# A streaming decode kernel: six transfers joined to their neighbours

## The chip, the cores and the metric

One core of one Trainium2 chip runs the whole program; the other cores are not used. The metric is the device time of one execution in microseconds (us). Everything is float32. The core's engines are TensorE (PE in the profile, PEld for its weight loads), VectorE (DVE), ScalarE (ACT), GpSimd (POOL) and SyncE (SP); SP's queue issues all large transfers from HBM to the on-chip buffer.

## The reference

Four sequences, one new token each, width 640. Two attention layers and two MLPs alternate, and both attention layers use the same weights and caches, as both MLPs do:

```
x = x + A(layernorm(x))      # layer one
x = x + B(layernorm(x))
x = x + A(layernorm(x))      # layer two, same W_q, K, V, W_o
x = x + B(layernorm(x))

A(x):  q = x @ wq                       # 640 -> 32 heads of 128
       k, v = the last 1024 cached positions of each head
       p = softmax(q k^T / sqrt(128));  o = p v
       return o @ wo                    # 4096 -> 640
B(x):  return (relu(x @ W_gate) * (x @ W_up)) @ W_down   # 640 -> 1728 -> 640
```

Keys and values differ for each of the four sequences, so each element of the caches is used once in a layer. A layer's caches and weights don't fit on the chip together, so nearly all of them are read from HBM twice.

## The kernel before

**One buffer, one stream.** `store` is one tile of 128 partitions by 50624 columns. The inputs lie in HBM as three matrices of 128 rows: `heads` (what 27 heads need, 255744 columns: W_q, K, V and W_o in the order of use), `kept` (the same for the other five heads, 47360 columns) and `mlp` (25920 columns). A load copies a stretch of columns of one of them to a place in `store`; one column is 512 bytes. The heads are worked off in nine groups (`HEADS`: six of four, two of three, one of two). The last two groups, K0 and K1 (heads 27 to 29, and 30 and 31), are the five kept heads: they are done last in layer one, stay in `store` while the MLP's weights pass through what is free, and are done first in layer two, where they are not read again.

**The plan.** `plan` is a list of loads written out by `put` and `stretch` when the program is made: matrix, columns from and to, place. It holds, in this order: the common heads of layer one; with them, at column 3200 of `store`, the 3200 columns of W_q of the kept heads (`put(0, "kept", KEPT * D, ...)`, line 164), then the last three loads of common heads (line 165); the kept heads; the MLP of layer one, in a ring of small places (`gu` twice, `gu_end`, `wd`, lines 170 to 178); the first loads of layer two, into places that the kept heads leave (lines 182 to 189); the common heads of layer two (lines 191 to 203); its MLP in eight loads (`cuts`, line 204). No load is wider than `MOST`, 16320 columns.

**What sets the order.** All loads are issued by SP in the order of the plan. `load()` issues the next one at the point in the program at which `done` has marked its whole place as free; on the chip SP then waits until PE has truly read what lay there. Eight semaphores are used in turn for these loads, so that a load also waits for the landing of the one eight before it. PE goes through its matrix products in program order, each reading a stretch of `store` once that stretch's load has landed: a load is one unit, and none of it counts as there before the last byte is.

**An attention layer** (`attention`) interleaves groups: totals and transposed probabilities of group g, the query of the group after next (`query`), scores of the next group (`scores`), the output projection of the group before (`project`), values of g (`values`). All matrix products go through `product`, line 252: `m` is a query, `ps` scores, `po` values, `y` the residual stream, `pp` the MLP's gate and up columns. An MLP (`forward`) computes the hidden columns in four tiles, `gate(3)`, `gate(0)`, `gate(1)`, `gate(2)` (1920, 5120, 5120 and 5120 columns of the matrix), with the activation `gated` between them, then `down(3)`, `down(0)`, `down(1)`, `down(2)`.

Of the kernel before, what the change touches and what calls it, by code (L numbers as in the profile page):

```python
# [13 lines left out]
B, D, H, DH, W, F = 4, 640, 32, 128, 1024, 1728  # L14
# [17 lines left out]
KEPT = len(HEADS[K0]) + len(HEADS[K1])  # L32
# [19 lines left out]
GU0, GU = KC * 3 * P, KC * 4 * 256  # L52
WD0 = GU0 + 3 * GU
TAIL, WD1, WD = WD0 + D, WD0 + D + 2 * QUARTER, 4 * D
MLP = WD1 + 3 * WD
# [6 lines left out]
STORE = 50624  # L62
FRONT = KEPT * 2 * (D + KV)


AHEAD = KEPT * D, KEPT * D + 768
BACK = FRONT - 2 * KV - 1728, FRONT - 2 * KV
AWAY = BACK[0] - 1280, BACK[0]
HOME = 12864
FIRST, MOST = 32640, 16320  # L70
# [7 lines left out]
def fewest(lo, end, n):  # L78

    if n == 1:  # L80
        return (0, [end]) if end - lo <= MOST else (n + len(CUTS), [])
    most = min(lo + MOST, end)
    ends = [(most, most not in CUTS)] + [(x, False) for x in CUTS if most - 512 < x < most]
    return min((fewest(hi, end, n - 1)[0] + cut, [hi, *fewest(hi, end, n - 1)[1]]) for hi, cut in ends)


def spread(parts):


    at, places, cuts = 0, {}, [0]  # L90
    for what, i in parts:
        places[what, i] = at
        size = size_of(what, i)
        step = {"q": size // KC, "k": 512, "v": 512, "o": D}[what]
        cuts += range(at + step, at + size + 1, step)
        at += size
    return places, at, cuts


ROWS = {row: spread(parts) for row, parts in PARTS.items()}  # L100

CUTS = frozenset(ROWS["heads"][2])
fewest = cache(fewest)
WHERE = {part: (row, at) for row, (places, _, _) in ROWS.items() for part, at in places.items()}

# [2 lines left out]
def decode_kernel(ctx: ExitStack, tc: tile.TileContext, x, source, sel, out):  # L108
    nc = tc.nc
# [10 lines left out]
    store = big.tile([P, STORE], F32, name="store")  # L120
# [9 lines left out]
    def put(layer, row, to, *cuts):  # L130

        for lo, hi in zip(cuts, cuts[1:]):
            assert 0 < hi - lo <= MOST and to % 64 == lo % 64 == hi % 64 == 0 and to + hi - lo <= STORE, (row, lo, hi, to)
            plan.append((layer, row, lo, hi, to))
            to += hi - lo
        return to

    def stretch(layer, lo, end, to):

        for hi in fewest(lo, end, -(-(end - lo) // MOST))[1]:  # L140
            if to + hi - lo > LAP:
                to = 0
            to = put(layer, "heads", to, lo, hi)
            lo = hi
        return to
# [4 lines left out]
    def near(c, row="heads"):  # L150

        return max(x for x in ROWS[row][2] if x <= c)

    heads_end = ROWS["heads"][1]
# [3 lines left out]

    q_end = 2 * KEPT * D
    turn = min(c for c in ROWS["heads"][2] if c >= heads_end - (STORE - q_end))  # L160
    mid = [near(turn + (heads_end - turn) * i // 3) for i in (1, 2)]
    to = stretch(0, HELD, turn, FIRST)
    assert to <= KEPT * D or to > 2 * MOST, to
    put(0, "kept", KEPT * D, KEPT * D, q_end)
    put(0, "heads", q_end, turn, *mid, heads_end)
    put(0, "kept", k0, k0, k1, v0, v0 + 6656, v1, v1 + KV, v1 + 7168, FRONT)
    put(0, "kept", 0, 0, len(HEADS[K0]) * D, KEPT * D)


    f, z, a, q, k = FRONT, STORE - D, AHEAD[0], AWAY[0], BACK[0]  # L170
    assert STORE - FRONT == 2 * 1280 + 64 + D
    gu = [(z, D), (f, 1280), (f + 1280, 1344), (a, 768), (k, 960), (k + 960, 768), (q, 1280)]
    gu_end = [(f, 1280), (f + 1280, 1280), (f + 2560, D)]
    wd = [(a, D), (k, 960), (k + 960, D), (q, 1280), *gu_end, (a, D), (k, D), (k + D, D)]
    lo = 0
    for to, n in gu + gu + gu_end + wd:
        put(0, "mlp", to, lo, lo + n)
        lo += n
    assert lo == MLP
# [2 lines left out]
    lo = HELD  # L182
# [1 line left out]
        put(1, "heads", to, lo, lo + n)  # L184
        lo += n
    to = AHEAD[1]
    for n in 1152, 1280, 1024, 2048, 3392:
        to = put(1, "heads", to, lo, lo + n)
        lo += n
    assert to == HOME  # L190
    to = HOME + BACK[1] - BACK[0]
    for n in 4096, 6144, 9728:
        hi = near(lo + n)
        to = put(1, "heads", to, lo, hi)
        lo = hi
    hi = near(lo + 4608)
    to = put(1, "heads", to, lo, hi)
    lo, hi = hi, near(hi + STORE - to)
    put(1, "heads", to, lo, hi)
    last = near(heads_end - 25216)  # L200
    to = stretch(1, hi, last, 0)
    for lo, hi in (last, near(last + 12800)), (near(last + 12800), heads_end):
        to = put(1, "heads", to if to + hi - lo <= STORE else 0, lo, hi)
    cuts = [0, 7040, 12160, GU0 + 3 * GU, WD1 + WD, MLP - 4 * D, MLP - 2 * D, MLP - D, MLP]
    for lo, hi in zip(cuts, cuts[1:]):
        to = put(1, "mlp", to if to + hi - lo <= STORE else 0, lo, hi)

# [2 lines left out]
    live = [False] * STORE  # L210
    held = {}

    def load():

        if not held:
            nc.sync.dma_start(out=first_q, in_=source["heads"][:, :HELD])
        while plan and not any(live[plan[-1][4]:plan[-1][4] + plan[-1][3] - plan[-1][2]]):
            layer, row, lo, hi, to = plan.pop()
            live[to:to + hi - lo] = [True] * (hi - lo)
            held.setdefault((layer, row), []).append((lo, hi - lo, to))  # L220
            nc.sync.dma_start(out=store[:, to:to + hi - lo], in_=source[row][:, lo:hi])

    def free(a, b):
        live[a:b] = [False] * (b - a)
        load()
# [29 lines left out]
    def done(layer, row, lo, n):  # L255

        if row == "kept" and layer == 0:
            return
        if row == "kept":
            for p in range(lo, lo + n):  # L260
                if BACK[0] <= p < BACK[1]:
                    live[HOME + p - BACK[0]] = False
                elif not (AHEAD[0] <= p < AHEAD[1] or HOME <= p < HOME + BACK[1] - BACK[0]):
                    live[p] = False
        else:
            for first, m, p in held[key(layer, row)]:
                a, b = max(lo, first) - first, min(lo + n, first + m) - first
                if a < b:
                    live[p + a:p + b] = [False] * (b - a)
        load()  # L270
# [8 lines left out]

    probs = work.tile([P, W], F32, name="probs")  # L280
    load()
    gates = work.tile([P, 512], F32, name="gates")
    sel_sb = const.tile([P, P + 32], F32, name="sel_sb")
# [390 lines left out]
```

## Time and profile before

| | |
|---|---|
| median of 3 runs | 732.04 us (731.85 to 732.34) |
| span of the profiled execution, first to last instruction | 729.8 us |
| what lies around the span, by the median | 2.2 us |
| PE busy | 437.2 us (60%) |
| DVE busy, ACT busy | 76.7 us (11%), 54.2 us (7%) |
| transfers of SP's queue | 310.56 MB |
| mean rate over the span | 426 GB/s |
| mean granted TensorE clock | 0.822 |

The profiled execution gives a span; its own time is taken as the span and the 2.2 us around it, which is the median. The spread of the three runs is 0.5 us, 0.07%.

In rows of the timeline the columns are start, duration, engine, source line, operation, output and inputs, partitions and elements, count; in brackets the engine's idle time before the row and what ended it. In a row on a transfer the last number is the time from its issue to its landing. Four bytes times 128 partitions make 512 bytes a column, so 640 columns are 320 KB.

### The profile page before, as it was taken

The page shows a single profiled execution, that of the slowest core. Times are in us where ns is not written, and L with a number is a line of the kernel's source. Part 1 is how long each engine was busy: PE and PEld are TensorE (multiplying, and loading weights), DVE is VectorE, ACT ScalarE, POOL GpSimd, SP SyncE. Part 2 cuts the span into 40 slices and gives each one's busy share as a digit, 9 for nine tenths or more (in the row PEclk, how much of TensorE's full clock was granted, in tenths as well). Part 3 has the DMA queues.
Part 4 walks back from the last instruction along what each step waited for, and adds up shares of the span by engine and source line. Part 5 has one row for each costly group of instructions (what it writes and reads, how often), then busy time and mean ns, then how long its engine had stood idle before and what let it go on. Part 6 is the DMA issues. An engine that isn't in the chain of part 4 may idle for free.

```text
span 729.8 us, 8270 instructions
## 1 busy us (share of the span) xinstructions
PE 437.2 (60%) x3764; PEld 143.9 (20%) x3764; DVE 76.7 (11%) x277; ACT 54.2 (7%) x101; POOL 0.3 (0%) x5
## 2 busy tenths in 40 slices
PE   0745565555646664619868896365656556555575
PEld 0211111111111111103333241021111112111132
DVE  1111001010010101001111211001010010101011
ACT  0200000000000000000412210000000000000100
POOL 0000000000000000000000000000000000000000
PEclk9888888876777777759999999677777777878899
DMA  9999999999999999999999999999999999999996
GB/s 409 442 398 443 442 443 416 438 440 439 418 439 432 411 460 421 447 416 426 419 407 401 434 429 449 445 425 435 425 435 443 429 434 427 441 433 430 421 425 289
DMA packets 13290, 311.17 MB, mean 426 GB/s; under 512 B 1476, under 2 KB 1732, under 8 KB 6984
## 3 DMA queue, kind: packets, MB, share of 16 engines
q1 hardware_dynamic: 13104, 310.56, 99.0%
q8 instruction: 29, 0.48, 0.2%
q10 hardware_dynamic: 152, 0.09, 0.1%
q14 instruction: 5, 0.04, 0.0%
HBM read 310.57 MB, written 0.08 MB: 426 GB/s over the span
## 4 chain that ended last, share of the span: by engine, by line
DMA 76%; PE 21%; another core or an unknown queue 1%; DVE 1%; issue 1%; SPq 0%; ACT 0%; DVEq 0%; ACTq 0%
DMA store<-in_heads 60%; PE ps L252 9%; DMA store<-in_kept 8%; DMA store<-in_mlp 7%; PE po L252 5%; PE m L252 2%; PE y L252 1%; PE pp L252 1%; PE pp L432 1%; PE m L403 1%; PE m L472 0%; PE m L463 0%; PE m L345 0%; PE y L375 0%
## 5 line engine op out<-in xcount | busy, mean ns | idle before, releaser
L252 PE MATMUL po<-store,pT 128*16 128x512 f32 (+1 forms) x1026 | 155.3, 709 | 123.6 <-DMA store<-in_heads 118.2
L252 PE MATMUL ps<-store,qT 128*4 128x512 f32 (+4 forms) x996 | 150.4, 684 | 109.8 <-DMA store<-in_heads 89.2
L252 PEld LDWEIGHTS po<-store,pT 128*16 128x16 f32 x1026 | 34.2, 109 | 230.3 <-issue 109.2
L252 PEld LDWEIGHTS ps<-store,qT 128*4 128x4 f32 x996 | 29.9, 93 | 213.4 <-DMA store<-in_heads 100.3
L424 DVE TENSOR_REDUCE nm<-ps 128x1 f32<-128x1024 f32 x17 | 20.8, 1225 | 240.7 <-PE ps L252 240.7
L428 ACT ACTIVATE probs<-ps,nm 128x1024 f32<-128x1024 f32 x17 | 18.9, 1114 | 327.0 <-DVE nm L424 327.0
L252 PE MATMUL m<-store,xT 128*32 128x512 f32 (+4 forms) x150 | 28.4, 570 | 11.0 <-DMA store<-in_heads 11.0
L442 DVE COPY pT<-pp 128x16 f32<-128x16 f32 x128 | 17.1, 169 | 137.8 <-PE po L252 137.8
L252 PE MATMUL y<-store,oT 128*4 128x160 f32 x514 | 22.6, 307 | 9.9 <-DMA store<-in_heads 8.7
L459 ACT COPY gates<-po 128x512 f32<-128x512 f32 x16 | 9.4, 587 | 252.4 <-PE po L252 252.4
L252 PE MATMUL pp<-store,xT 128*32 128x256 f32 (+3 forms) x322 | 20.1, 350 | 8.7 <-DMA store<-in_mlp 4.3
L432 PE MATMUL pp<-sel_sb,probs 128*128 128x128 f32 x144 | 20.7, 291 | 0.0
L465 DVE RECIPROCAL r<-m 128x16 f32<-128x16 f32 x18 | 4.6, 258 | 132.9 <-PE m L463 132.9
L432 PEld LDWEIGHTS pp<-sel_sb,probs 128*128 128x128 f32 x144 | 18.3, 153 | 0.0
L252 PEld LDWEIGHTS y<-store,oT 128*4 128x4 f32 x514 | 12.7, 88 | 17.5 <-DMA store<-in_heads 9.1
L396 DVE TENSOR_SCALAR gates<-m,rstd 128x512 f32<-128x512 f32 (+2 forms) x18 | 12.4, 690 | 24.9 <-PE m L252 24.9
L252 PEld LDWEIGHTS pp<-store,xT 128*32 128x32 f32 x322 | 10.3, 109 | 17.0 <-DMA store<-in_mlp 7.7
L472 PE MATMUL m<-sel_sb,gates 128*128 128x128 f32 x72 | 11.9, 287 | 0.8 <-DVE gates L452 0.8
L403 PE MATMUL m<-sel_sb,gates 128*128 128x128 f32 x64 | 12.3, 315 | 0.0
L322 PE MATMUL y<-probs,sel_sb 4*4 4x160 f32 x8 | 0.7, 444 | 18.2 <-DMA sel_sb<-in_sel 18.2
L403 PEld LDWEIGHTS m<-sel_sb,gates 128*128 128x128 f32 x64 | 7.6, 155 | 18.3 <-issue 17.9
L252 PE MATMUL y<-store,gates 128*4 128x160 f32 x192 | 9.6, 299 | 2.5 <-DMA store<-in_mlp 2.3
(74 smaller groups left out, 126.1 us busy)
## 6 DMA issues: line engine op xcount, KB each, us to landing
store<-in_heads SPq DMA_DIRECT2D x17, 7936.0 KB, 46.1
store<-in_heads SPq DMA_DIRECT2D x2, 8160.0 KB, 44.7
store<-in_heads SPq DMA_DIRECT2D x2, 8128.0 KB, 36.1
store<-in_heads SPq DMA_DIRECT2D x2, 7968.0 KB, 36.1
store<-in_heads SPq DMA_DIRECT2D x1, 8096.0 KB, 26.4
store<-in_heads SPq DMA_DIRECT2D x1, 7424.0 KB, 44.9
store<-in_heads SPq DMA_DIRECT2D x1, 7360.0 KB, 35.8
store<-in_heads SPq DMA_DIRECT2D x1, 7168.0 KB, 34.0
```

The lines of the kernel that those rows point to most:

```text
L252: nc.tensor.matmul(out[:, a:z], by, t[rows, p:p + z - a], start=start and not a, stop=stop and z == n, **how)
L322: nc.tensor.matmul(y[32 * g:32 * g + B], ident[:B, :B], probs[:B, g * QUARTER:(g + 1) * QUARTER], start=True, stop=True, tile_position=(0, ...
L396: nc.vector.tensor_scalar(gates[:, :len(HEADS[g]) * P], qp.pop(g), rstd, SCALE, op0=ALU.mult, op1=ALU.mult)
L403: nc.tensor.transpose(qt[:, i], gates[:, i * P:(i + 1) * P], ident)
L424: nc.vector.tensor_reduce(nm[g], to.rearrange("p j n -> p (j n)"), axis=AX.X, op=ALU.max, negate=True)
L428: nc.scalar.activation(probs, sc.pop(g).rearrange("p j n -> p (j n)"), AF.Exp, bias=nm.pop(g), accum_out=sums[g])
L432: nc.tensor.transpose(pp[:, c // 4, c % 4 * P:c % 4 * P + P], probs[:, c * P:(c + 1) * P], ident)
L442: nc.vector.tensor_copy(to[:, 4 * j:4 * j + 4], pp[:, j].rearrange("p (c x) -> p c x", c=4)[:, :, i:P:32])
L459: nc.scalar.copy(gates, po)
L465: nc.vector.reciprocal(r[g], so.rearrange("p (b i) -> p i b", b=B)[:, :SIDE])
L472: nc.tensor.transpose(ot[:, 127 * b:127 * b + P], gates[:, b * P:(b + 1) * P], ident)
```

## The change

Six loads are joined to neighbours; the same bytes go to `store`.

1. W_q of the kept heads (3200 columns) is now also laid into the matrix `heads`, between the last loads of layer one's common heads (`QUERIES` holds the place in the matrix and the size), and comes in one load with the 12288 columns of heads behind it. The three loads of common heads at that point become 15488 (with W_q), 15488 and 16128 columns. The matrix `heads` has 258944 columns instead of 255744, that is 1035776 bytes a row instead of 1022976.
2. The first lap of the MLP's ring in layer one has five loads, 1920, 1344, 768, 1728 and 1280 columns, instead of seven (640, 1280, 1344, 768, 960, 768, 1280); the second lap has seven as before, starting at the ring's front instead of its end.
3. In layer two's first loads 1152 and 1280 become 2432, and 1024 and 2048 become 3072.
4. In layer two's MLP 7040 and 5120 become 12160. Among the last common heads of layer two 16320, 15936 and 12800 become 13824, 15872 and 15360, as many as before.

```diff
+QUERIES = min(c for c in CUTS if c >= ROWS["heads"][1] - (STORE - 2 * KEPT * D)), KEPT * D
 ...
-    mid = [near(turn + (heads_end - turn) * i // 3) for i in (1, 2)]
+    mid = [near(turn + (heads_end - turn + QUERIES[1]) * i // 3 - QUERIES[1]) for i in (1, 2)]
 ...
-    put(0, "kept", KEPT * D, KEPT * D, q_end)
     put(0, "heads", q_end, turn, *mid, heads_end)
 ...
-    f, z, a, q, k = FRONT, STORE - D, AHEAD[0], AWAY[0], BACK[0]
+    f, a, q, k = FRONT, AHEAD[0], AWAY[0], BACK[0]
-    gu = [(z, D), (f, 1280), (f + 1280, 1344), (a, 768), (k, 960), (k + 960, 768), (q, 1280)]
-    gu_end = [(f, 1280), (f + 1280, 1280), (f + 2560, D)]
+    gu = [(f, 1920), (f + 1920, 1344), (a, 768), (k, 1728), (q, 1280)]
+    gu += [(f, D), (f + D, 1280), (f + 1920, 1344), (a, 768), (k, 960), (k + 960, 768), (q, 1280)]
+    gu += [(f, 1280), (f + 1280, 1280), (f + 2560, D)]
 ...
-    for n in 1152, 1280, 1024, 2048, 3392:
+    for n in 2432, 3072, 3392:
 ...
-    last = near(heads_end - 25216)
-    to = stretch(1, hi, last, 0)
-    for lo, hi in (last, near(last + 12800)), (near(last + 12800), heads_end):
+    to = stretch(1, hi, turn, 0)
+    last, end = near(turn + MOST), near(heads_end - 12608)
+    for lo, hi in (turn, last), (last, end), (end, heads_end):
 ...
-    cuts = [0, 7040, 12160, GU0 + 3 * GU, WD1 + WD, MLP - 4 * D, MLP - 2 * D, MLP - D, MLP]
+    cuts = [0, GU0 + 2 * GU, GU0 + 3 * GU, WD1 + WD, MLP - 4 * D, MLP - 2 * D, MLP - D, MLP]
 ...
-            nc.sync.dma_start(out=store[:, to:to + hi - lo], in_=source[row][:, lo:hi])
+            at, n = lo, hi - lo
+            if row == "heads" and lo >= QUERIES[0]:
+                at += QUERIES[1]
+            if (layer, row, lo) == (0, "heads", QUERIES[0]):
+                at, n, to = at - QUERIES[1], n + QUERIES[1], to - QUERIES[1]
+                ...
+            nc.sync.dma_start(out=store[:, to:to + n], in_=source[row][:, at:at + n])
 ...
+    at, size = QUERIES
+    queries = laid["kept"][:, KEPT * D:KEPT * D + size]
+    laid["heads"] = np.concatenate([laid["heads"][:, :at], queries, laid["heads"][:, at:]], axis=1)
```

SP's queue at the end of layer one's common heads, before (a load's matrix, and partitions by columns):

```order
L221 DMA store<-in_heads 128x16256
L221 DMA store<-in_heads 128x15872 x2
L221 DMA store<-in_kept 128x3200
L221 DMA store<-in_heads 128x14336
L221 DMA store<-in_heads 128x14720
L221 DMA store<-in_heads 128x14848
L221 DMA store<-in_kept 128x12288
```

and after:

```order
L231 DMA store<-in_heads 128x16256
L231 DMA store<-in_heads 128x15872 x2
L231 DMA store<-in_heads 128x15488 x2
L231 DMA store<-in_heads 128x16128
L231 DMA store<-in_kept 128x12288
```

Four loads of 47104 columns have become three; the first of them now brings W_q of the kept heads and 12288 columns of heads as one unit. The start of layer two's ring in SP's queue, before:

```order
L221 DMA store<-in_heads 128x1728
L221 DMA store<-in_heads 128x1152
L221 DMA store<-in_heads 128x1280
L221 DMA store<-in_heads 128x1024
L221 DMA store<-in_heads 128x2048
L221 DMA store<-in_heads 128x3392
```

and after:

```order
L231 DMA store<-in_heads 128x1728
L231 DMA store<-in_heads 128x2432
L231 DMA store<-in_heads 128x3072
L231 DMA store<-in_heads 128x3392
L231 DMA store<-in_heads 128x4096
```

Each joined load stands where its second half stood, and can be issued when the places of both halves are free. The end of SP's queue, the last heads and the MLP of layer two, before:

```order
L221 DMA store<-in_heads 128x12672
L221 DMA store<-in_mlp 128x7040
L221 DMA store<-in_mlp 128x5120 x2
L221 DMA store<-in_mlp 128x3520
L221 DMA store<-in_mlp 128x2560
```

and after:

```order
L231 DMA store<-in_heads 128x12672
L231 DMA store<-in_mlp 128x12160
L231 DMA store<-in_mlp 128x5120
L231 DMA store<-in_mlp 128x3520
L231 DMA store<-in_mlp 128x2560
```

`gate(3)`, `gate(0)` and `gate(1)` of layer two now read one load; before, the first two read the first load and `gate(1)` the second. On PE the instructions keep their order; three products that were split at a border between two loads (columns 512 as 448 and 64, 192 and 320, 448 and 64) are whole, and DVE, ACT and POOL have the same rows.

More of the change, by code (lines that the diff above doesn't have):

```diff
@@ L160, in decode_kernel @@
     turn = min(c for c in ROWS["heads"][2] if c >= heads_end - (STORE - q_end))
-    mid = [near(turn + (heads_end - turn) * i // 3) for i in (1, 2)]
+    mid = [near(turn + (heads_end - turn + QUERIES[1]) * i // 3 - QUERIES[1]) for i in (1, 2)]
+    assert (turn, q_end - KEPT * D) == QUERIES
     to = stretch(0, HELD, turn, FIRST)
     assert to <= KEPT * D or to > 2 * MOST, to
-    put(0, "kept", KEPT * D, KEPT * D, q_end)
     put(0, "heads", q_end, turn, *mid, heads_end)
@@ L167, in decode_kernel @@
     put(0, "kept", 0, 0, len(HEADS[K0]) * D, KEPT * D)
-    f, z, a, q, k = FRONT, STORE - D, AHEAD[0], AWAY[0], BACK[0]
+    f, a, q, k = FRONT, AHEAD[0], AWAY[0], BACK[0]
     assert STORE - FRONT == 2 * 1280 + 64 + D
-    gu = [(z, D), (f, 1280), (f + 1280, 1344), (a, 768), (k, 960), (k + 960, 768), (q, 1280)]
-    gu_end = [(f, 1280), (f + 1280, 1280), (f + 2560, D)]
-    wd = [(a, D), (k, 960), (k + 960, D), (q, 1280), *gu_end, (a, D), (k, D), (k + D, D)]
+    gu = [(f, 1920), (f + 1920, 1344), (a, 768), (k, 1728), (q, 1280)]
+    gu += [(f, D), (f + D, 1280), (f + 1920, 1344), (a, 768), (k, 960), (k + 960, 768), (q, 1280)]
+    gu += [(f, 1280), (f + 1280, 1280), (f + 2560, D)]
+    wd = [(a, D), (k, 960), (k + 960, D), (q, 1280), *gu[-3:], (a, D), (k, D), (k + D, D)]
     lo = 0
-    for to, n in gu + gu + gu_end + wd:
+    for to, n in gu + wd:
         put(0, "mlp", to, lo, lo + n)
@@ L220, in load @@
             held.setdefault((layer, row), []).append((lo, hi - lo, to))
-            nc.sync.dma_start(out=store[:, to:to + hi - lo], in_=source[row][:, lo:hi])
+            at, n = lo, hi - lo
[3 more added lines that the diff above has]
+                at, n, to = at - QUERIES[1], n + QUERIES[1], to - QUERIES[1]
+                assert to == KEPT * D and n <= MOST and not any(live[to:to + QUERIES[1]])
+                live[to:to + QUERIES[1]] = [True] * QUERIES[1]
+                held.setdefault((layer, "kept"), []).append((to, QUERIES[1], to))
+            nc.sync.dma_start(out=store[:, to:to + n], in_=source[row][:, at:at + n])
     def free(a, b):
```

## The prediction

> **What bounds the kernel.** I read the page's transfer rows first, then the chain of work that ended last, then the core's transfers in single stretches, and last PE's timeline around each joined load.
>
> ```profile
> span 729.8 us, 8270 instructions
> DMA  9999999999999999999999999999999999999996
> q1 hardware_dynamic: 13104, 310.56, 99.0%
> DMA 76%; PE 21%; another core or an unknown queue 1%; DVE 1%; issue 1%; SPq 0%; ACT 0%; DVEq 0%; ACTq 0%
> ```
>
> The 16 DMA engines are busy in every slice but the last, and SP's queue (q1) alone fills 99.0% of their time. The chain gives 21% to PE, but during PE's pieces of it the DMA engines were busy too: those pieces decide when a load may be issued, not when the stream of bytes ends. So the time is the length of one unbroken stream: start, 310.56 MB and whatever each load costs beside its bytes, then a fixed end. The end hangs on the last load:
>
> ```profile
> 695.60 30.68 DMA store<-in_mlp
> ```
>
> It was issued at 695.60 and landed at 726.28, and almost all of those 30.68 us are other loads ahead of it. A change can act in two ways: make the stream cheaper, or break it. The bytes stay the same.
>
> **The price of a load.** No row has it alone, so I take stretches from the transfers' view: the common heads from 20 to 220 us, layer one's MLP from 366 to 396 us, the start of layer two from 396 to 406 us (all queues for the first two, then q1 alone for all three), and beside them a load with nothing ahead of it, the output:
>
> ```profile
> DMA packets 1536, 86.51 MB, mean 433 GB/s; under 512 B 176, under 2 KB 176, under 8 KB 176
> DMA packets 3536, 12.17 MB, mean 406 GB/s; under 512 B 393, under 2 KB 393, under 8 KB 3531
> q1 hardware_dynamic: 1529, 86.40, 99.8%
> q1 hardware_dynamic: 3531, 12.10, 101.2%
> q1 hardware_dynamic: 985, 4.02, 101.3%
> out_x<-probs SPq DMA_DIRECT2D x1, 80.0 KB, 1.6
> ```
>
> The page's 13104 packets on q1 are those of 91 loads, 144 each, so the stretches hold 10.6, 24.5 and 6.8 loads. With x us a MB and c us a load, 200 = 86.51 x + 10.6 c and 30 = 12.17 x + 24.5 c give x = 2.30 (434 GB/s) and c = 0.08. The third, 10 = 4.02 x + 6.8 c, gives c = 0.11. The ends: nothing, if the shortfall in small loads belongs to the place and not to the load (less than nothing is excluded, since the same bytes in fewer loads give the engines no work; later issues are counted below); and 1.4 us, the output's 1.6 less 0.2 for its bytes, if the stream stood still for each load's latency. I take 0.08, which is the value that the two longest stretches share, and stay far from 1.4, since 24.5 loads at that price are 34 us in a stretch of 30 that also moved its bytes. **Six loads fewer save 0.5 us** (0 to 0.7 by 0.11).
>
> The Trainium skill (DMA: Bandwidth & Descriptors, "Anatomy of one DMA") gives each DMA a fixed cost of about 2.0 us. Taken as additive, six would be an estimated 12 us and the time 720; the stretch of 24.5 loads in 30 us disagrees, so nearly all of that cost lies beside other loads here.
>
> **W_q of the kept heads with the last common heads (one load).** The query that needs it ran long before its data will now land:
>
> ```profile
> 263.47 1.16 PE L252 MATMUL m<-store,xT 128*32 128x384 f32 x9
> 264.57 2.09 PE L252 MATMUL ps<-store,qT 128*4 128x512 f32 x13
> 275.37 5.46 PE L252 MATMUL ps<-store,qT 128*4 128x512 f32 x32 [8.71 <-DMA store<-in_heads]
> 326.19 4.37 PE L252 MATMUL ps<-store,qT 128*4 128x512 f32 x20 [20.58 <-DMA store<-in_kept]
> 258.35 0.33 SPq L221 DMA_DIRECT2D store<-in_heads  x1
> store<-in_heads SPq DMA_DIRECT2D x1, 7360.0 KB, 35.8
> ```
>
> Before, 3200 and 14336 columns landed one after the other, the second for PE's start at 275.37. The joined load is 2048 columns shorter than both, 1.05 MB or 2.4 us, so it lands at about 272.9. PE's work from 263.47 to 266.66 moves behind that, 3.2 us, and the 5.5 us of scores follow: 281.6 instead of 280.8. What the scores' first third frees, the place of the third load of common heads, comes 10 us later, at about 276; the load ahead of it, issued at 258.35, lands at 294.2 (35.8 later), so 18 us of queue remain. PE's 0.8 us vanish in its wait of 20.58 us at 326.19. Cost 0; without that cover 0.8. The place itself is asked for no later than before: the joined load needs 12288 columns of heads free where the old one needed 14336.
>
> **The first lap of the ring (two loads).** The pair 960 and 768 is the one that waits for something late, its second half's place, issued at 362.66:
>
> ```profile
> 362.66 0.33 SPq L221 DMA_DIRECT2D store<-in_mlp  x1
> store<-in_mlp SPq DMA_DIRECT2D x1, 384.0 KB, 8.3
> 346.42 0.81 SPq L221 DMA_DIRECT2D store<-in_mlp  x2
> store<-in_mlp SPq DMA_DIRECT2D x1, 640.0 KB, 19.5
> 366.48 1.18 PE L252 MATMUL pp<-store,xT 128*32 128x128 f32 x27 [0.46 <-DVE xT L359]
> 371.03 0.63 PE L252 MATMUL pp<-store,xT 128*32 128x256 f32 x6 [0.35 <-DMA store<-in_mlp]
> 372.58 1.05 PE L252 MATMUL pp<-store,xT 128*32 128x256 f32 x10 [0.92 <-DMA store<-in_mlp]
> ```
>
> The load issued there landed 8.3 us later, 0.9 of it its own bytes. With the output's 1.4 us for latency, 6.0 us are queue: the first half can be issued that late without a gap. On PE the first 960 columns now count as landed only with the other 768, about 1 us later; PE waits up to 1 us more before 371.03, and then less in the 0.92 us before 372.58. The other joined load (640 and 1280, now 1920) lands with its second half, at 366.3 (19.5 after its issue, the later of the two from 346.42 to 347.23), before PE's first product at 366.48. Cost 0.
>
> **The start of layer two (two loads).** Here the queue is shortest, so this is where the stream could break:
>
> ```profile
> 399.00 0.33 SPq L221 DMA_DIRECT2D store<-in_heads  x1
> 399.81 0.33 SPq L221 DMA_DIRECT2D store<-in_heads  x1
> 401.63 0.33 SPq L221 DMA_DIRECT2D store<-in_heads  x1
> 402.49 0.33 SPq L221 DMA_DIRECT2D store<-in_heads  x1
> store<-in_heads SPq DMA_DIRECT2D x1, 576.0 KB, 5.3
> store<-in_heads SPq DMA_DIRECT2D x1, 512.0 KB, 5.4
> ```
>
> The first halves move from 399.00 to 399.81 and from 401.63 to 402.49, 0.8 and 0.9 us later. They landed after 5.3 and 5.4 us; less 1.4 of their own bytes and 1.4 of latency (1.2 and 1.4) that leaves 2.5 and 2.8 us of queue ahead. So 1.7 and 1.9 us stay. Cost 0; if the queue were empty there, 0.8 + 0.9 = 1.7 us. Nobody waits early for the data: it is for group 0's scores, two groups on.
>
> **Layer two's MLP (one load) and last heads.** `gate(3)` needs the first 1920 columns and will have to wait for 12160:
>
> ```profile
> 707.11 1.18 PE L252 MATMUL pp<-store,xT 128*32 128x128 f32 x27 [0.47 <-DVE xT L359]
> 672.19 0.33 SPq L221 DMA_DIRECT2D store<-in_mlp  x1
> store<-in_mlp SPq DMA_DIRECT2D x1, 2560.0 KB, 37.7
> 720.15 0.84 PE L252 MATMUL y<-store,probs 128*4 128x160 f32 x16 [1.58 <-DMA store<-in_mlp]
> 723.35 1.27 PE L252 MATMUL y<-store,gates 128*4 128x160 f32 x32 [1.16 <-DMA store<-in_mlp]
> 724.89 1.11 PE L252 MATMUL y<-store,gates 128*4 128x160 f32 x24 [0.28 <-DMA store<-in_mlp]
> 726.32 0.46 PE L252 MATMUL y<-store,gates 128*4 128x160 f32 x8 [0.33 <-DMA store<-in_mlp]
> 695.58 7.00 PE L252 MATMUL po<-store,pT 128*16 128x512 f32 x42 [3.95 <-DMA store<-in_heads]
> ```
>
> The second half (2560 KB, issued at 672.19) landed at 709.9. Before, `gate(3)` began at 707.11, when the layer norm was done; now it begins 2.8 us later, and the chain of gates behind it shifts as a whole. Cover: PE's four waits for data behind the gates, 1.58 + 1.16 + 0.28 + 0.33 = 3.35 us. They hold 2.8 and leave 0.5. Cost 0, but this is the thinnest cover of the change; with no cover at all the end would come 2.8 us later. The resized last heads put 2560 columns into the load before the last, five products of 0.34 us (5.46 us for 32 half products), under the wait of 3.95 us at 695.58. The three unsplit products save PE some tenths off the path: 0.
>
> **Sum.** 0.5 us less on the stream, 0 from the rest: span 729.8 to 729.3, with the 2.2 us around it 731.5; against the median, 732.04 - 0.5 = **731.5 us**, 0.07% less. A measurement of this kernel can tell about 0.2%, 1.5 us, from no change.
>
> **Rivals.** *The tail turns PE-bound* (slower): `gate(3)`'s 2.8 us come through to the end. For it: the cover exceeds the delay by 0.5 us only, and PE's chain of gates has no other slack. Against: four rows of waits. It decides from where over 2.0 of the 2.8 us (1.5 + 0.5) stay uncovered; in full, 732.04 + 2.8 - 0.5 = 734.3.
>
> *Layer two's ring runs dry:* both late issues leave the engines without work, +1.7, so 733.2. For it: the stretch is the slowest per byte (0.11 a load), a sign of a short queue. Against: 1.7 us left in it.
>
> *The whole shortfall of 366 to 406 us was a short queue, and wider loads cure it* (faster): 12.17 and 4.02 MB at 2.30 take 37.2 of 40 us, so up to 2.8 less, 729.2. Against: only four of its 31 loads go, and the queue's depth there stays.
>
> *Each load's latency is paid by the stream* (faster): 6 x 1.4 = 8.4 us, 723.6. Against: the 34 us above.
>
> *The wider rows of `heads` read slower* (slower): each row starts 1035776 instead of 1022976 bytes after the last. It takes 2.0 us of some 600 us of heads to matter, 0.33%; 1% gives +6.0 - 0.5, 737.5. Against: in the stretch of `kept`, with rows of 189440 bytes, the rate is near that of `heads`:
>
> ```profile
> 325.00:360.00 35.00, 30.80 (x286) 10.12 (x288) 5.54 (x25) 7.18 (x11) 0.00 (x0) 0.92 1.00 426
> ```
>
> The Trainium skill (DMA: Bandwidth & Descriptors, "Latency and other measured facts") has a loss at row pitches of large powers of two, 164 instead of 214 GB/s at 2 MiB, and none once 4 MiB was padded by 4 KiB; 1035776 is 12800 bytes short of 1 MiB, and no run here shows the effect.
>
> **Chances.** Forecast 0.83; ring dry 0.05; tail 0.04; shortfall cured 0.05; rows 0.02; latency paid 0.01. The forecast and the dry ring lie within 0.2%: same 0.88; faster 0.06; slower 0.06. The range: down, six loads at 0.11 and half the runs' spread, 732.04 - 0.7 - 0.3 = 731.0, and 0.3 more for a part of the cure, 730.7; up, nothing saved, the spread and part of a gap or of the tail, 732.04 + 0.3 + 0.3 = 732.6.
>
> **What would show it.** Right: 85 loads, so about 12240 packets on q1; the same shares of the DMA engines; PE's wait for heads near 273 instead of 275; `gate(3)` begun at about 709.5 after a wait for `in_mlp`, and PE still waiting for data in `down`; the last load landing at about 725.8. Wrong: a slice between 390 and 410 us with DMA engines under nine tenths; no wait for data in `down(2)`; fewer GB/s from 20 to 220 us.

## The result: slower by 0.4%, and the profile after

The changed kernel took **734.23 us** (median of 5 runs, 733.72 to 736.13) against 732.04 us (731.62 to 732.34) for the kernel before on the same chip: ratio 1.0037, interval 1.0026 to 1.0047. The whole interval lies above 1, so the change is slower, and the time is 1.6 us above the forecast range. The profiled execution has a span of 732.0 us instead of 729.8.

The lines of the page of the changed kernel that answer to those of before:

```profile
span 732.0 us, 8247 instructions
DMA  9999999999999999999999999999999999999996
q1 hardware_dynamic: 12240, 310.56, 98.8%
DMA 76%; PE 21%; DVE 1%; issue 1%; ACT 0%; SPq 0%; DVEq 0%
```

12240 packets are 85 loads, six fewer, with the same bytes. The DMA engines are as full as before, and the chain's shares of DMA and PE are the same to the per cent: by the page's summary nothing happened. The difference stands in the chain in order of time, here its last 61 us in the changed kernel (start, duration, what):

```profile
671.04 39.81 DMA store<-in_mlp
710.85 0.14 issue
710.99 1.52 PE pp L262 x25
...
714.23 4.35 PE pp L262 x40
...
719.46 2.41 PE pp L262 x40
...
722.70 2.37 PE pp L262 x40
725.06 4.07 PE y L262 x112
```

Before, this stretch was one row, the last load from 695.60 to 726.28, with half a microsecond of PE behind it. Now the chain leaves the stream at 710.85, when the joined load of 12160 columns lands, and runs through PE to the end: the tail has turned PE-bound. SP's row for the output, after:

```profile
729.54 0.35 SPq L626 DMA_DIRECT2D out_x<-probs  x1
```

and before:

```profile
727.24 0.35 SPq L616 DMA_DIRECT2D out_x<-probs  x1
```

It comes 2.30 us later. The last load landed at 727.45 instead of 726.28 (1.17 us later), and the output left 2.09 us behind that landing instead of 0.96 (1.13 us more). So in this execution about half of the loss is in the stream of bytes, half in PE's tail. The stream's half reaches PE through the joined load: it landed at 710.85, and its second half alone had landed at 709.90 before. PE's timeline after shows the other half:

```profile
707.16 0.49 PE L346 MATMUL po<-sel_sb 128*128 128x128 f32 x2
710.99 1.72 PE L262 MATMUL pp<-store,xT 128*32 128x128 f32 x27 [3.34 <-DMA store<-in_mlp]
714.23 4.35 PE L262 MATMUL pp<-store,xT 128*32 128x256 f32 x40 [0.42 <-DVE gates L565]
719.46 2.37 PE L262 MATMUL pp<-store,xT 128*32 128x256 f32 x40 [0.55 <-DVE probs L565]
722.70 2.37 PE L262 MATMUL pp<-store,xT 128*32 128x256 f32 x40 [0.88 <-DVE probs L565]
725.65 3.44 PE L262 MATMUL y<-store,gates 128*4 128x160 f32 x96
```

and before, the row of `gate(0)`:

```profile
709.72 2.37 PE L252 MATMUL pp<-store,xT 128*32 128x256 f32 x40 [0.81 <-DVE gates L555]
```

`gate(3)` waits 3.34 us for `in_mlp`, as the change makes it. But then the 40 products of `gate(0)`, 2.37 us before, take 4.35 us, and `down` runs through without a wait for data: the cover has been used up. The stretches of the changed kernel tell why (columns: stretch and its length, busy time and count of PE, PEld, DVE, ACT and POOL, granted TensorE clock, share of the DMA engines, GB/s):

```profile
402.00:406.00 4.00, 4.00 (x40) 0.99 (x36) 0.15 (x1) 1.72 (x3) 0.00 (x0) 1.00 0.98 354
711.00:714.00 3.00, 2.81 (x40) 2.39 (x40) 0.27 (x2) 0.57 (x2) 0.00 (x0) 0.58 0.99 427
714.00:719.00 5.00, 4.68 (x48) 2.09 (x48) 0.22 (x2) 0.35 (x1) 0.00 (x0) 0.57 1.00 423
```

and the same three of before:

```profile
402.00:406.00 4.00, 4.00 (x44) 1.00 (x36) 0.04 (x1) 1.73 (x3) 0.00 (x0) 1.00 1.02 416
711.00:714.00 3.00, 2.46 (x50) 1.38 (x44) 0.75 (x3) 0.37 (x1) 0.00 (x0) 1.00 0.96 407
714.00:719.00 5.00, 3.69 (x68) 1.73 (x56) 0.66 (x2) 0.73 (x2) 0.00 (x0) 1.00 0.99 421
```

Behind PE's stand (the time in which it has nothing to run) the granted clock is 0.58 and 0.57 where it was 1.00; below, "half clock" means the stretches in which the records grant 0.50. The first row of each is the stream's half of the loss: at the start of layer two the stream moved 354 GB/s for 4 us instead of 416, at nearly the same share of the engines (0.98 and 1.02). Matched by bytes delivered, the stream after was 0.15 us ahead at 393 us, 0.2 us behind at 402 and 0.8 us behind at 406, and 0.7 to 0.8 us behind from there to the end. Only the step from 402 to 406 us stands out: at 402, five of the kernels below that keep the old order of these loads lay between 0.3 us ahead and 0.6 us behind as well.

### The profile page after: what moved, and what is told of

It is laid out like the page before. It is cut to its first block, busy times and chain, and to the rows that moved or that the text cites. A ratio compares the mean times of both kernels' runs of the same rounds, so it can differ in the third digit from the quotient of the medians.

```text
span 732.0 us, 8247 instructions
## 1 busy us (share of the span) xinstructions
PE 442.4 (60%) x3758; PEld 144.9 (20%) x3758; DVE 76.6 (10%) x277; ACT 54.2 (7%) x101; POOL 0.3 (0%) x5
## 3 DMA queue, kind: packets, MB, share of 16 engines
q1 hardware_dynamic: 12240, 310.56, 98.8%
## 4 chain that ended last, share of the span: by engine, by line
DMA 76%; PE 21%; DVE 1%; issue 1%; ACT 0%; SPq 0%; DVEq 0%
DMA store<-in_heads 58%; DMA store<-in_mlp 10%; PE ps L262 8%; DMA store<-in_kept 8%; PE po L262 6%; PE pp L262 2%; PE m L262 2%; PE y L262 1%; PE pp L442 1%; PE m L413 0%; DVE nm L434 0%; PE m L482 0%; PE m L473 0%; PE y L385 0%; ACT gates L564 0%
## 5 line engine op out<-in xcount | busy, mean ns | idle before, releaser
L262 PE MATMUL ps<-store,qT 128*4 128x512 f32 (+3 forms) x990 | 151.2, 693 | 102.5 <-DMA store<-in_heads 79.9
L262 PE MATMUL pp<-store,xT 128*32 128x256 f32 (+3 forms) x322 | 23.0, 387 | 10.8 <-DMA store<-in_mlp 7.3
L262 PEld LDWEIGHTS m<-store,xT 128*32 128x32 f32 x150 | 6.4, 118 | 32.7 <-issue 19.9
```

The source lines that it names most:

```text
L262: nc.tensor.matmul(out[:, a:z], by, t[rows, p:p + z - a], start=start and not a, stop=stop and z == n, **how)
```

## The experiments

Three theories. *Clock*: PE's stand ahead of `gate(3)` brings the half clock, and that, not the delay, uses up the cover. *Delay alone* (rival): the delay was larger than the cover, at whatever clock. *Stream*: the joined loads at the start of layer two cost time in the stream, whatever the tail does. Each kernel below ran 11 or 12 times, and each ratio is to the kernel before on the same chip (732 us there). The prediction's base, the kernel before, had a spread of about 1 us over more than 30 runs.

### Undoing one part or both

Edit to the changed kernel for the first (layer two's MLP cut as before):

```diff
-    cuts = [0, GU0 + 2 * GU, GU0 + 3 * GU, WD1 + WD, MLP - 4 * D, MLP - 2 * D, MLP - D, MLP]
+    cuts = [0, 7040, 12160, GU0 + 3 * GU, WD1 + WD, MLP - 4 * D, MLP - 2 * D, MLP - D, MLP]
```

> The changed kernel with layer two's MLP loaded in 7040 and 5120 columns again instead of 12160 (5 loads fewer than before). Changed kernel 734.2, before 732.0. Theory A, two places: the late gates of layer two's MLP cost 1.1 to 2 us (PE idles 3.3 us at 707.6 and then runs at half clock), the joined loads at the start of layer two cost the stream 0.9. Then here 732.6 to 733.0: gate(3) starts at the layer norm's end without a wait for in_mlp, no half clock behind it, the last load still lands near 727.4. Theory B, tail alone: 731.6. Theory C, stream alone (PE's tail is late only because the stream is): 734.2. Theory D, the wider rows of heads read slower: 734.2.

Edit for the second (the start of layer two as before):

```diff
-    for n in 2432, 3072, 3392:
+    for n in 1152, 1280, 1024, 2048, 3392:
```

> The changed kernel with the first loads of layer two as 1152, 1280, 1024 and 2048 columns again (4 loads fewer than before). Theory A: the stream is 0.9 us faster from 406 us on (last load at about 726.3 to 726.5), gate(3) of layer two still waits some 3 us and the gates still run at half clock, 733.0 to 733.6. Theory B: 734.2. Theory C: 731.7. Theory D: 734.2.

The third has both edits, so that W_q, the first lap and the resized last heads are left of the change:

> The changed kernel with both undone: only W_q of the kept heads and the ring's first lap of five loads stay (3 loads fewer than before). Theories A, B and C: 0.08 us a load, 731.8, last load at 726.0. Theory D: 734 (the rows of heads are as wide as in the changed kernel).

Measured: tail undone 732.37 us, ratio 1.0003 (0.9995 to 1.0012); ring undone 731.79, 1.0002 (0.9993 to 1.0010), with 3 of 11 executions at 732.9 to 733.8; both undone 732.2, 1.0002 (0.9993 to 1.0012). The first two are faster than the theory of two places (A) gave, 732.6 to 733.0 and 733.0 to 733.6. With the tail undone the last load of the profiled execution lands at 727.28 us and the output follows 0.95 us behind it: a late stream without PE's loss. The median of all its runs shows 0.4 us of that, which cannot be told from nothing. W_q, the first lap and the last heads cost and gain nothing that can be measured. Undoing either part takes away nearly the whole loss, so the loss is not a plain sum. PE's timeline with the ring undone gives a part of the reason:

```profile
710.30 1.18 PE L262 MATMUL pp<-store,xT 128*32 128x128 f32 x27 [2.23 <-DMA store<-in_mlp]
712.90 3.48 PE L262 MATMUL pp<-store,xT 128*32 128x256 f32 x40 [0.64 <-DVE gates L565]
...
720.50 2.37 PE L262 MATMUL pp<-store,xT 128*32 128x256 f32 x40 [0.87 <-DVE probs L565]
```

The joined load lands 0.7 us earlier than in the changed kernel (710.16 instead of 710.85). PE also comes to the stand 0.4 us later (708.06 instead of 707.65): behind its wait for the last heads half clock lasted 6.8 us here and 3.4 in the changed kernel, and the same 42 products took 8.13 us instead of 7.02. So PE stands 2.23 us instead of 3.34, and `gate(0)` is slow only in part (3.48 us). A late stream lengthens the stand, a late PE shortens it; with one trace of each kernel, how often each happens stays open.

### Joining the tail alone

Edit to the kernel before:

```diff
-    cuts = [0, 7040, 12160, GU0 + 3 * GU, WD1 + WD, MLP - 4 * D, MLP - 2 * D, MLP - D, MLP]
+    cuts = [0, GU0 + 2 * GU, GU0 + 3 * GU, WD1 + WD, MLP - 4 * D, MLP - 2 * D, MLP - D, MLP]
```

> The kernel before with the one edit of layer two's MLP, 12160 columns in one load instead of 7040 and 5120. Theory A: the stream as before (last load at 726.2), gate(3) late by 2.8 us, half clock behind it, 733.1 to 734. Theory B: 734.2. Theory C: 732.0, since PE's waits behind the gates cover 3.35 us.

Measured: 733.03 us (732.08 to 735.53), ratio 1.0017 (1.0008 to 1.0027). PE's timeline:

```profile
710.01 1.91 PE L252 MATMUL pp<-store,xT 128*32 128x128 f32 x27 [3.45 <-DMA store<-in_mlp]
713.44 4.17 PE L252 MATMUL pp<-store,xT 128*32 128x256 f32 x40 [0.42 <-DVE gates L555]
...
724.67 3.44 PE L252 MATMUL y<-store,gates 128*4 128x160 f32 x96
```

Here the stream was on time (last landing at 726.19, before 726.28), and `gate(3)` began 2.9 us later than before, which is the delay that the prediction gave it. Still the time grew by 1.1 us: this part is enough to cost time by itself. PE stood longest of all here, with no late stream, because it came early, at 706.57.

### Taking away the stand, not the delay

`fill(n)` issues products of the identity into a bank that nobody reads until it is overwritten, the device that the kernel already has to keep PE busy; `fill(12)` shows as 24 products in PE's timeline. Edit to the changed kernel, in `forward`:

```diff
+        if layer:
+            fill(12)
         gate(3)
```

> The changed kernel with 12 idle products (identity by identity into an unused bank) on PE ahead of gate(3) of layer two, so that PE doesn't stand still while the 12160 columns land. Changed kernel 734.2. Clock theory: the wait itself is covered, the half clock that follows it is not; with it gone the gates take 2.4 us each again, PE waits for in_mlp in down, the end hangs on the last load, which the joined ring loads keep 1.0 us late: 732.4 to 732.8, with the spread of the runs back under 1 us. Delay theory: the late start of gate(3) alone makes the tail PE-bound: 734.2 or more.

The same two lines in the changed kernel with the ring undone, and in the kernel with the tail alone:

> The changed kernel with the ring's joined loads undone and the 12 idle products ahead of gate(3) of layer two: four loads fewer than before and no half clock at the end. Clock theory with a price of 0.05 us a load (1.5 us for 32 loads): 731.7 to 731.9, and none of the slow outliers of the same kernel without the products (731.5 to 733.8, three of eleven over 732.9). Delay theory: 732.5 or more.

> The kernel before with layer two's MLP in the 12160 load and the 12 idle products: without the products 733.0, 1.1 over before. Clock theory: 731.9 to 732.1, the cover of 3.35 us that was worked out beforehand holds once the gates run at full clock. Delay theory: 733.0.

PE's timeline of the changed kernel with `fill(12)`:

```profile
707.76 3.17 PE L346 MATMUL po<-sel_sb 128*128 128x128 f32 x26
710.86 1.18 PE L262 MATMUL pp<-store,xT 128*32 128x128 f32 x27
...
713.47 2.37 PE L262 MATMUL pp<-store,xT 128*32 128x256 f32 x40 [0.81 <-DVE gates L565]
...
726.72 0.46 PE L262 MATMUL y<-store,gates 128*4 128x160 f32 x8 [0.33 <-DMA store<-in_mlp]
```

and of the tail alone with it:

```profile
710.87 1.18 PE L252 MATMUL pp<-store,xT 128*32 128x128 f32 x27 [1.41 <-DMA store<-in_mlp]
...
713.47 2.37 PE L252 MATMUL pp<-store,xT 128*32 128x256 f32 x40 [0.80 <-DVE gates L555]
...
727.10 0.46 PE L252 MATMUL y<-store,gates 128*4 128x160 f32 x8 [0.30 <-DMA store<-in_mlp]
```

In both, `gate(3)` begins about as late as without the fill or later (710.86 against 710.99, and 710.87 against 710.01). The granted clock is 1.00 from 711 to 719 us, the 40 products of each of `gate(0)` to `gate(2)` take 2.37 us, and the last 8 products still wait for data. The output follows the last landing (726.67 and 727.05) by 0.96 us, as in the kernel before. The time falls with it: tail alone 731.94 (731.61 to 732.51), ratio 0.9999 (0.9991 to 1.0008), where it was 1.0017; the whole change 732.27 (731.4 to 733.45), 1.0004 (0.9995 to 1.0013), where it was 1.0037, and 1.0019 in the second measurement below; ring undone 731.71 (731.49 to 732.04), 0.9995 (0.9987 to 1.0004), with no execution above 732.04. More work on PE, at no less delay, is faster. That separates the clock from the delay alone. One expectation failed: the whole change with the fill still spreads over 2 us instead of under 1, where the other two with it spread over 0.5 and 0.9 us. So a part of the spread of the whole change comes from elsewhere than the stand (the joined loads at the start of layer two alone, below, spread over 1.6 us).

### Half the fill, and the change once more

The first has `fill(6)` in place of `fill(12)`; the second is the changed kernel without an edit.

> The changed kernel with 6 idle products, so that PE stands still for about 1.7 us instead of 3.3 ahead of gate(3). If half clock follows only a long stand: as with 12 products, 732.3. If any stand of this size brings it: 734.2. In between, 733, if it comes in some executions and not in others.

> The changed kernel once more, beside the others on this chip, for its spread and a second profile. Clock theory: 733.7 to 736, half clock from about 711 us for 3 to 7 us, the end set by PE. If the first profile was an exception: 732.5.

Measured: half the fill 732.34 us (731.63 to 735.16), ratio 1.0007 (0.9998 to 1.0015); the change again 733.39 (732.49 to 734.9), 1.0019 (1.0011 to 1.0028), slower once more, by less. The profiled execution of the half fill happens to be its slowest, 735.16:

```profile
711.03 1.18 PE L262 MATMUL pp<-store,xT 128*32 128x128 f32 x27 [3.09 <-DMA store<-in_mlp]
...
713.63 4.49 PE L262 MATMUL pp<-store,xT 128*32 128x256 f32 x40 [0.45 <-DVE gates L565]
...
719.18 3.98 PE L262 MATMUL pp<-store,xT 128*32 128x256 f32 x40 [0.53 <-DVE probs L565]
```

and its clock, in single microseconds:

```profile
712.00:713.00 1.00, 1.00 (x19) 0.78 (x13) 0.16 (x1) 0.30 (x2) 0.00 (x0) 0.64 0.97 417
...
722.00:723.00 1.00, 1.00 (x16) 0.32 (x8) 0.00 (x0) 0.00 (x0) 0.00 (x0) 0.74 0.94 387
```

PE stood 3.09 us and not the 1.7 that was expected, since it came early here (its row ahead of the stand began at 706.11, in the changed kernel at 707.16). So this trace doesn't test a short stand. `gate(3)` still ran at full clock, then the half clock lasted from about 712.3 to 722.5 and took in two gates. In the repeat of the change it began earlier, at about 710.4 (a clock of 0.68 from 710 to 711), slowed `gate(3)` too (2.14 us) and ended at about 717.2, so that `gate(0)` took 3.55 us only. The same stand thus costs another amount in each execution, by where the half clock begins and how long it lasts. I read the slowest executions of the kernels with the stand (735.5 for the tail alone, 736.1 for the change) from that; only one execution of each has a trace, so it is not shown.

### The start of layer two

Edits to the kernel before: the two joined loads alone,

```diff
-    for n in 1152, 1280, 1024, 2048, 3392:
+    for n in 2432, 3072, 3392:
```

> The kernel before with only the first loads of layer two joined (2432 and 3072 for 1152, 1280, 1024 and 2048). Theory A1, the late issues leave DMA engines without work: the 2432 load lands about 1.7 us late, the stream stays 0.6 to 1.0 us late to the end, 732.6 to 732.9. Rival, the step of 0.9 us at 395 to 406 us is scatter between executions: 731.9.

and, with no load joined, the halves of each pair in the other order, so that the queue gets its first bytes of a pair as late as with the join (the places in `store` stay):

```diff
+    plan[-5:-1] = plan[-4], plan[-5], plan[-2], plan[-3]
```

> The kernel before with the same four loads at the start of layer two in the order 1280, 1152, 2048, 1024 instead of 1152, 1280, 1024, 2048: each pair is then issued when both places are free, as a joined load is, but as two loads. Theory A1 (lateness): the stream loses what it loses in the joined form, 0.6 to 1.0 us, 732.6 to 732.9. Theory A2 (the size of the joined load, not its time of issue): 731.9.

Measured: joined alone 732.23 us, ratio 1.0006 (0.9997 to 1.0015); swapped 732.49, 1.0008 (0.9999 to 1.0017). Neither can be told from no change, and both lie between what the two theories gave. The traces tell more. From 402 to 406 us, ring alone:

```profile
402.00:406.00 4.00, 4.00 (x44) 1.00 (x36) 0.04 (x1) 1.72 (x3) 0.00 (x0) 1.00 1.02 391
```

halves swapped:

```profile
402.00:406.00 4.00, 4.00 (x40) 0.99 (x36) 0.09 (x1) 1.72 (x3) 0.00 (x0) 1.00 1.00 400
```

ring undone, with the fill:

```profile
402.00:406.00 4.00, 4.00 (x44) 1.02 (x36) 0.01 (x1) 1.72 (x3) 0.00 (x0) 1.00 1.01 415
```

The six profiled kernels with the two joined loads moved 342 to 398 GB/s here (mean 371), the seven that have the four loads in the old order 403 to 421 (mean 412). 41 of 412 GB/s over 4 us are 0.4 us. Matched by bytes delivered, the six fell back against the kernel before by 0.26 to 0.79 us between 402 and 406 us, those with the old order by 0.03 at most. So the join does cost the stream about 0.4 us here. The swapped order fell back by 0.1 us in its one trace, which speaks against lateness as the whole cause, though its time is no better than that of the join; whether by lateness or by the size of the load stays open.

### The price of a load

Edit to the kernel before: each of the 32 loads wider than 8192 columns is issued as two halves, one behind the other.

> The kernel before with each of its 32 loads over 8192 columns issued as two halves at the same point: 32 loads more, all where the queue is deep. Price 0.08 us a load: 734.5. Price 0: 732.0. Price 0.11: 735.5. Latency paid by the stream, 1.4 us a load: 777.

Measured: 733.39 us (733.18 to 733.57), ratio 1.0020 (1.0011 to 1.0029). 32 more loads cost 1.46 us, 0.046 us each (0.025 to 0.066 by the interval), and the trace has the stream 1.6 us behind at 720 us. So at that price six loads fewer are worth 0.28 us.

## Why the prediction was wrong, and where it was right

**The step that failed: "They hold 2.8 and leave 0.5."** The delay was as forecast where the stream was on time (2.9 us with the tail alone), and at full clock the cover holds even 3.75 us (710.86 against 707.11 with the fill, and 0.33 us of wait left; the last load landed 0.4 us later there, which widens the cover by as much). But the gates' durations were taken from rows with a granted clock of 1.00 and used behind a stand that the change itself made: `gate(3)` and the 40 products behind it then took 2.5 us more (1.72 and 4.35 instead of 1.18 and 2.37 us), and with the 3.9 us of delay here that is 6.4 us against a cover of 3.35. That leaves 3.05 us; PE made up 0.75 of it between its products and in `down`, which ran without a stop, and the output left 2.3 us later. The sum counted the wait's length and not what the wait does to the engine. The kernel before shows it too, in a row that the prediction quotes: at the end of the wait of 3.95 us, at 695.58, half clock begins, and the granted clock is 0.50 from 696 to 698 us.

The Trainium skill (TensorE: Matmul & The Clock Gate, "HAM oscillation — how this bites in real kernels") says that a wait for a DMA of over about 3.4 us returns PE to half clock. The stands of 3.34 and 3.45 us here, with granted clocks of 0.58 and 0.50 from 711 to 714 us, are of about that length and agree. Those of 2.23 and 3.09 us are shorter, and half clock followed them too. Weighed against the wait of some 3 us that the prediction itself gave `gate(3)`, that rule would have spoken for much more than 0.04.

**The rival that came true** is the tail that turns PE-bound, at 0.04, 734.3 us. Place and sign were right and its number is 0.1 us off, but by chance (the change once more took 733.39): its mechanism was 2.8 us of delay without cover, "PE's chain of gates has no other slack". The runs with the fill show the delay to be free. What came in its place is 1.1 us of PE's tail at half clock, and the stream's loss.

**The start of layer two, "Cost 0": wrong by about 0.4 us, by the traces.** The times of this part alone don't tell it from nothing. The last landing in the profiled execution is 1.17 us late; of that the stream's lag at 406 us explains 0.7 to 0.8, and 0.6 of it came between 402 and 406. The cushion of 1.7 and 1.9 us was worked from landings, which are the last byte of a whole load, and says nothing of one of the 16 engines that has emptied its part earlier; whether one had, no run shows. Rival "runs dry" had the place; its mechanism is not seen: the queue ahead of the joined loads was 3.6 and 5.0 us by the landings, and the engines count as busy all through. The late stream also moves the joined load: `gate(3)` came at 710.99 instead of the forecast 709.5.

**The price of a load, 0.08 us: too high.** By the split it is 0.046, and 0.08 lies outside the interval of 0.025 to 0.066; so the shortfall of the stretches with small loads belongs in part to their place, if small loads cost what the split's large ones do. The saving forecast as 0.5 us is then 0.3, and no trace shows it: at 393 us, with three of the six loads gone, eight kernels lay between 0.22 us ahead of the kernel before and 0.10 behind, and four that still had all three lay 0.12 to 0.34 ahead. The Trainium skill (DMA: Bandwidth & Descriptors, "Anatomy of one DMA") gives the 2.0 us a DMA that the prediction names as a fit for transfers on GpSimd's path. SP's loads are on the queue that the profile calls `hardware_dynamic`, and the 0.046 us is for them.

**W_q with the last common heads, 0: right.** PE's row for the joined load, after:

```profile
273.04 2.10 PE L262 MATMUL m<-store,xT 128*32 128x384 f32 x9 [10.08 <-DMA store<-in_heads]
...
325.89 5.65 PE L262 MATMUL ps<-store,qT 128*4 128x512 f32 x36 [22.60 <-DMA store<-in_kept]
```

Forecast 272.9, and the cover at 326.19 was there, now 22.60 us at 325.89. **The first lap, 0: right**, PE's waits became

```profile
370.95 1.06 PE L262 MATMUL pp<-store,xT 128*32 128x192 f32 x14 [0.58 <-DMA store<-in_mlp]
372.46 1.05 PE L262 MATMUL pp<-store,xT 128*32 128x256 f32 x10 [0.45 <-DMA store<-in_mlp]
```

in place of 0.35 and 0.92 us, the exchange that was described, and smaller. **The wider rows of `heads`**: no loss, 433 GB/s from 20 to 220 us before and after. **The rival of the latency of each load**, 8.4 us for six, fell with the split: 32 loads more would have cost 45 us, not 1.5.

Of the signs named, "no wait for data in `down(2)`" was the one that showed. "A slice under nine tenths" could not have shown the stream's loss, since the share was still 0.98 while the rate fell to 354 GB/s.

## What to carry to other kernels

When a change makes PE wait somewhere new, price the work behind that wait at half clock as well as at full clock, and compare the cover with both; if PE has to stand some 2 us or more ahead of work that decides the end, let it run products that nobody reads (in these traces half of the stands of 2.2 to 2.9 us brought half clock, and every one from 3.0 us on). Where a queue is short, don't prove a cushion by landings or by the busy share of the DMA engines: compare bytes per time in the stretch. With the fill, and the start of layer two left as it was, the other four joins are harmless (731.71 us, ratio 0.9995, 0.9987 to 1.0004), but at 0.05 us a load there was nothing to win that could be measured.

## What the runs showed of the hardware

- At the end of layer two half clock came after stands of PE of 2.23, 3.09, 3.34 and 3.45 us, not after one of 1.41 us. It began between about 0.7 us before PE's next product (the repeat of the change) and 1.2 to 1.5 us behind it (half fill, ring undone). It lasted about 3.4 us (ring undone), 6.8 (the change, its repeat and the tail alone) and 10.2 (half fill).
- Length alone doesn't decide it. Counted over all 14 traces from 20 us on, for stands that began at full clock and half clock that began during them or within 2 us behind them: it came after none of 66 stands of 1.0 to 1.8 us, after 10 of 20 of 2.2 to 2.9 us, and after all 423 of 3.0 us or more. In the kernel with the split loads a stand of 2.55 us left `gate(2)` at its 2.37 us:

```profile
717.62 2.37 PE L255 MATMUL pp<-store,xT 128*32 128x256 f32 x40 [2.55 <-DMA store<-in_mlp]
```

- A load's fixed cost, 0.046 us in this full queue, is far below the 1.4 us that the output, a lone small transfer, takes beside its bytes.
- The busy share of the DMA engines hardly falls where they move less: 0.98 at 354 GB/s and 1.02 at 416 for the same four microseconds. In the records of single packets of the changed kernel, the packets of the two joined loads took 0.37 and 0.46 us at the median, but 14 of the 256, all in the first half of their load, took 0.6 to 1.7 us, and that time counts as busy.
